# First batch of a fused attention and feed-forward kernel: attention times v in float32, shared exponentials, normalising on GpSimd, and weights converted in wider steps

## The chip, the cores and the metric

The kernel runs on one core of one Trainium2 chip. The metric is the device time of one launch in microseconds (us). Engines are called as the profile calls them: PE (TensorE, the matrix engine), PEld (its weight load), DVE (VectorE), ACT (ScalarE), POOL (GpSimd) and SP (SyncE, which only issues DMAs here).

## The reference

Attention with keys and values averaged over 8 neighbours, then a two-layer feed-forward net with a leaky ReLU. `q`, `k` and `v` are float32 [8 batches, 8 heads, 576, 64]; the weights are float64, 512 x 2048 and 2048 x 512.

```python
k_p = k.reshape(B, H, Sp, 8, D).mean(axis=3)          # Sp = 72
v_p = v.reshape(B, H, Sp, 8, D).mean(axis=3)
scores = (1 / sqrt(D)) * matmul(q, k_p.transpose(0, 1, 3, 2))
scores = scores - max(scores, axis=-1)
attn = exp(scores);  attn = attn / (sum(attn, axis=-1) + 1e-09)
x = matmul(attn, v_p).transpose(0, 2, 1, 3).reshape(4608, 512)
h = x @ w_in
out = maximum(0.01 * h, h) @ w_out                    # 4608 x 512, float32
```

## The kernel before

**Feed-forward net.** Nine chunks of 512 tokens, 16 parts of 128 hidden units each. For a chunk and a part, `m1` makes 12 matmuls of 512 columns into `ph`, and `m2` 12 more into the four sums `acc`. Each float32 factor is a high and a low half (`xh`, `xl`; halves of the weights; `gh`, `gl`), and of the four products three are made. The chunk of batch 0 is begun with parts 0 to 7 (run 0), then comes all of batch 1's chunk (run 1), then batch 0's parts 8 to 15, then the rest. The first matmul of a part in run 0 needs all four full tiles of batch 0's attention.

**Weights.** They come as float64 and are rebuilt from their two 32-bit words (`bits`): two steps on ACT (L183, L184) and three on DVE (L185, L186, L189) give a float32 `t`; ACT casts the high half (L193) and DVE subtracts it for the low half (L194). `convert(i, f)` does it for part f, i = 0 for `w_in` and i = 1 for `w_out`, 512 elements in each partition, in two steps, `head` and `tail`. Words wait in the space of weights that are converted later (`spare`), `t` in a buffer with the tag `o`. `convert_to(n)` sets how many steps have been written out by a given point.

**Attention.** A batch has five tiles of queries (four of 128, one of 64) and two groups of four heads. The string `FIRST` is the order by hand for batch 0: `lk` and `lv` pool keys and values, `ku` and `vu` place them, `q2` transposes tile 2 of the queries, `sa21` makes scores, maxima and exponentials of tile 2, group 1, `sb21` its normalising, `pu21` its transposing into `pT`, `au01` attention times v of piece 0, group 1, and `c` is one conversion step. Batch 1 goes between the matmuls of run 0; its pooling is on POOL. Exponentials are four ACT instructions a group, one for each head, each with its sum. `pT` and `v` are split into halves, with four reduced-precision matmuls (L467 to L470) for each pair of heads. Tiles 2 and 3 of batch 0 are normalised on DVE (`NORM_DVE`), the others on POOL.

**Order.** PE's instructions stay in the order in which the program is written. On the other engines a scheduler orders them when the kernel is built, and from then on each engine works its own list in order.

Of the kernel before, what the change touches and what calls it, by code (L numbers as in the profile page):

```python
# [24 lines left out]
def tile_pooled_attention_ffn(  # L25
# [54 lines left out]
    four = ctx.enter_context(tc.tile_pool(name="four", bufs=4))  # L80
# [36 lines left out]
    v_lo = const.tile([P, NK, 2, D], F32R, name="v_lo")  # L117
# [25 lines left out]
    NORM_DVE = (2, 3)  # L143

    def spare(f, i, shape, dtype, name):

        return wts.tile(shape, dtype, tag=f"w{i}_{f}", name=name)

    def stage(f):

# [3 lines left out]
        for i in range(2):
            shape = [P, DM, 2]
            if slot > f:
                t = spare(slot, i, shape, I32, f"w{i}_bits{f}")
            else:
                t = two.tile(shape, I32, tag="raw", name=f"w{i}_bits{f}")
            if i == 0:  # L160
                nc.sync.dma_start(
                    t.rearrange("p (k f) w -> p k f w", k=NK), w_in[:, :, f * P : (f + 1) * P, :]
                )
            else:
                nc.sync.dma_start(t, w_out[:, f, :, :])
            bits[i, f] = t

    def convert(i, f):

        st = {}  # L170

        def head():
            b = bits.pop((i, f))
            low, high = b[:, :, 0], b[:, :, 1]
            ws[i, f] = spare(f, i, [P, 2, DM], F32R, f"w{i}_{f}")
            t = five.tile([P, DM], I32, tag="o", name=f"w{i}_t{f}")
            st["w"] = t.bitcast(F32)
# [13 lines left out]
        def tail():  # L191
            w, t = ws[i, f], st["w"]
            nc.scalar.copy(w[:, 0, :], t)  # L193
            nc.vector.tensor_tensor(w[:, 1, :], t, w[:, 0, :].bitcast(F32), op=ALU.subtract)  # L194
# [169 lines left out]
    def q_unit(b, t, qr):  # L364
# [5 lines left out]
        nc.scalar.copy(qT[:, :, :n], pq[:, :, :n])  # L370
# [15 lines left out]
    def s_unit(b, t, g, qT):  # L386
# [14 lines left out]
        nc.vector.tensor_reduce(out=mx[:n], in_=scv[:n], axis=AX.X, op=ALU.max, negate=True)  # L401
        for h in range(4):
            ins = nc.scalar.activation(  # L403
                e[:n, h, :], scv[:n, h, :], AF.Exp, bias=mx[:n, h : h + 1],
                accum_out=sm[:n, h : h + 1],
            )
# [4 lines left out]
    def norm_unit(b, t, g, e, sm):  # L411
        n = tiles[b][t][1]
        eng = nc.vector if b == 0 and t in NORM_DVE else nc.gpsimd
        nc.vector.tensor_scalar_add(sm[:n], sm[:n], 1e-9)
        nc.vector.reciprocal(sm[:n], sm[:n])  # L415
        at = wide(b, t, g, "at", [3, P]) if wide_at(b, t, "at") else three.tile([P, 3, P], F32, tag="at", name=f"at{b}_{t}_{g}")
        eng.tensor_tensor(  # L417
# [3 lines left out]
        ins = eng.tensor_tensor(  # L421
# [16 lines left out]
    def p_unit(b, t, g, at, pc, o):
# [5 lines left out]
        nc.scalar.copy(pc["hi"][:, :, o : o + n], pp[:, 0:2, :n])
# [11 lines left out]
    def av_unit(b, j, g, pc):  # L456
# [3 lines left out]
        for i in range(2):  # L460
# [7 lines left out]
            nc.tensor.matmul(pa, vh, pc["lo"][:, i, :w], start=False, stop=False)  # L468
            nc.tensor.matmul(pa, vl, pc["hi"][:, i, :w], start=False, stop=False)  # L469
# [204 lines left out]
    def m2(k):  # L674
# [176 lines left out]
```

## Time and profile before

| | |
|---|---|
| three runs | 1009.0, 1004.41, 1011.04 us; median 1009.0 |
| profiled execution | 1006.54 us, span 1004.8 us |
| busy share of the span | PE 95%, PEld 77%, DVE 37%, ACT 43%, POOL 18% |
| mean granted clock of PE | 0.982 |
| chain that ended last | PE 88%, DVE 5%, ACT 4% |
| DMA | 57.44 MB, mean 57 GB/s |

The profile has one execution. A row of the order of time is: start in us from the span's start, duration, engine, line, operation, what it writes `<-` what it reads, shapes, how many; in brackets the idle time before it and what ended that. Durations of neighbours on one engine overlap a little, so the price of an instruction in a dense stretch is the distance from one start to the next.

### The profile page before, as it was taken

How to read it: one execution, taken by the hardware profiler on the slowest of the kernel's cores; microseconds unless marked ns; L12 is line 12 of the kernel's file. 1: busy time of each engine (PE TensorE's matmuls, PEld its weight loads, DVE VectorE, ACT ScalarE, POOL GpSimd, SP SyncE). 2: the span in 40 equal slices, each digit the busy share in tenths (PEclk: the TensorE clock that was granted, in tenths of full speed). 3: DMA queues.
4: the chain of work that ended last, by engine and by line, in shares of the span. 5: the costliest groups of instructions: out<-in, count | busy, mean ns of one | idle time of the engine just before them, and what ended most of it. 6: DMA issues, size and time to landing. Idle time of an engine off the chain costs nothing.

```text
span 1004.8 us, 12738 instructions
## 1 busy us (share of the span) xinstructions
PE 952.5 (95%) x4536; PEld 778.1 (77%) x4536; DVE 371.5 (37%) x902; ACT 428.2 (43%) x1386; POOL 177.4 (18%) x292
## 2 busy tenths in 40 slices
PE   4468899999999999999999999999999999999998
PEld 3457678888787778888887888788877888788886
DVE  5998639323432322233232333233223322221111
ACT  4677766234433343434343434344443433322221
POOL 3602200401116610132013301220110100100000
PEclk9689999999999999999999999999999999999999
DMA  9955311312033400121022202110100010001001
GB/s 241 267 171 149 88 60 42 103 34 69 1 104 101 105 11 17 58 74 32 6 64 58 58 1 69 46 29 1 58 22 11 1 48 1 1 1 42 0 1 42
DMA packets 65006, 57.44 MB, mean 57 GB/s; under 512 B 39856, under 2 KB 48048, under 8 KB 64944
## 3 DMA queue, kind: packets, MB, share of 16 engines
q1 hardware_dynamic: 64944, 56.64, 19.8%
q8 instruction: 36, 0.59, 0.3%
q14 instruction: 26, 0.21, 0.1%
HBM read 46.14 MB, written 10.49 MB: 56 GB/s over the span
## 4 chain that ended last, share of the span: by engine, by line
PE 88%; DVE 5%; ACT 4%; issue 1%; DMA 1%; SPq 1%; POOL 0%; DVEq 0%; ACTq 0%; POOLq 0%
PE ph L661 13%; PE acc L685 13%; PE ph L663 13%; PE ph L662 13%; PE acc L687 13%; PE acc L686 13%; PE pss L393 4%; PE pp L442 3%; PE pq L368 1%; ACT e L403 1%; PE pa L468 1%; PE pa L467 1%; PE pa L470 1%; PE pa L469 1%; SPq L240 1%
## 5 line engine op out<-in xcount | busy, mean ns | idle before, releaser
L661 PE MATMUL ph<-xh,w 128*128 128x512 f32 x576 | 235.8, 409 | 0.0
L685 PE MATMUL acc<-w,gh 128*128 128x512 f32 x576 | 233.7, 406 | 0.0
L663 PE MATMUL ph<-xh,w 128*128 128x512 f32 x576 | 226.3, 393 | 0.0
L662 PE MATMUL ph<-xl,w 128*128 128x512 f32 x576 | 226.1, 393 | 0.0
L687 PE MATMUL acc<-w,gl 128*128 128x512 f32 x576 | 225.7, 392 | 0.0
L686 PE MATMUL acc<-w,gh 128*128 128x512 f32 x576 | 225.5, 392 | 0.0
L670 DVE TENSOR_TENSOR gl<-ph,gh 128x512 fp32r<-128x512 f32 x144 | 99.4, 690 | 263.2 <-ACT gh L669 262.3
L666 ACT ACTIVATE ph<-ph 128x512 f32<-128x512 f32 x144 | 84.2, 585 | 250.4 <-PE ph L663 250.3
L403 ACT ACTIVATE e<-pss,red 128x72 f32<-128x72 f32 (+1 forms) x320 | 98.2, 320 | 115.5 <-DVE red L401 115.3
L417 POOL TENSOR_TENSOR at<-e,red 128x256 f32<-128x256 f32 (+1 forms) x76 | 47.4, 624 | 543.7 <-DVE red L415 267.8
L663 PEld LDWEIGHTS ph<-xh,w 128*128 128x128 f32 x576 | 108.7, 189 | 24.0
L687 PEld LDWEIGHTS acc<-w,gl 128*128 128x128 f32 x576 | 108.4, 188 | 23.8
L685 PEld LDWEIGHTS acc<-w,gh 128*128 128x128 f32 x576 | 108.5, 188 | 22.3 <-issue 1.6
L661 PEld LDWEIGHTS ph<-xh,w 128*128 128x128 f32 x576 | 108.8, 189 | 21.9 <-issue 1.4
L686 PEld LDWEIGHTS acc<-w,gh 128*128 128x128 f32 x576 | 108.7, 189 | 19.7
L662 PEld LDWEIGHTS ph<-xl,w 128*128 128x128 f32 x576 | 108.9, 189 | 19.1
L669 ACT CAST gh<-ph 128x512 fp32r<-128x512 f32 x144 | 85.4, 593 | 3.1
L401 DVE TENSOR_REDUCE red<-pss 128x4 f32<-128x288 f32 (+1 forms) x80 | 36.1, 453 | 94.3 <-PE pss L393 93.2
L403 ACT ACTIVATION_READ_ACCUMULATOR e<-pss,red 128x1 f32 (+1 forms) x320 | 65.4, 204 | 0.0
L393 PEld LDWEIGHTS pss<-kT,qT 128*128 128x128 f32 (+1 forms) x320 | 47.1, 183 | 14.4 <-ACT qT L370 4.9
L393 PE MATMUL pss<-kT,qT 128*128 128x144 f32 (+1 forms) x320 | 53.8, 295 | 4.1 <-ACT qT L370 4.1
L448 DVE TENSOR_TENSOR pT_lo<-pp,pT_hi 128x256 fp32r<-128x256 f32 (+1 forms) x80 | 31.7, 396 | 66.0 <-ACT pT_rem L445 65.3
(93 smaller groups left out, 844.1 us busy)
## 6 DMA issues: line engine op xcount, KB each, us to landing
out_dram<-o SPq DMA_DIRECT2D x35, 256.0 KB, 2.9
q<-in_q_dram SPq DMA_DIRECT2D x32, 256.0 KB, 3.9
w_bits<-in_moe_w_in_dram SPq DMA_DIRECT2D x16, 512.0 KB, 3.7
w_bits<-in_moe_w_out_dram SPq DMA_DIRECT2D x16, 512.0 KB, 3.5
k0raw<-in_k_dram SPq DMA_DIRECT2D x16, 256.0 KB, 3.7
k1raw<-in_k_dram SPq DMA_DIRECT2D x16, 256.0 KB, 4.4
v0raw<-in_v_dram SPq DMA_DIRECT2D x16, 256.0 KB, 3.8
v1raw<-in_v_dram SPq DMA_DIRECT2D x16, 256.0 KB, 5.6
```

What stands on the lines that cost most here:

```text
L393: nc.tensor.matmul(sc[:n, 2 * SP * i : 2 * SP * (i + 1)], qT[:, p, :n], kT[:, p, :, :].rearrange("d i s -> d (i s)"), start=True, stop=True,)
L403: ins = nc.scalar.activation(e[:n, h, :], scv[:n, h, :], AF.Exp, bias=mx[:n, h : h + 1], accum_out=sm[:n, h : h + 1],)
L417: eng.tensor_tensor(at[:n, 0:2, :].rearrange("a i (h s) -> a (i h) s", h=2), e[:n, :, 0:MAIN], sm[:n].unsqueeze(2).broadcast_to([n, 4, MAI ...
L661: nc.tensor.matmul(ph, w[:, 0, ks], xh[kk], start=kk == 0, stop=False)
L662: nc.tensor.matmul(ph, w[:, 0, ks], xl[kk], start=False, stop=False)
L663: nc.tensor.matmul(ph, w[:, 1, ks], xh[kk], start=False, stop=kk == NK - 1)
L666: nc.scalar.activation(ph, ph, AF.Prelu, alpha=0.01)
L669: casts.append(nc.scalar.copy(gh, ph))
L670: nc.vector.tensor_tensor(gl, ph, gh.bitcast(F32), op=ALU.subtract)
L685: nc.tensor.matmul(a, gh[:, r], hi, start=first, stop=False)
L686: nc.tensor.matmul(a, gh[:, r], lo, start=False, stop=False)
L687: nc.tensor.matmul(a, gl[:, r], hi, start=False, stop=last)
```

## The change

All of it concerns batch 0 and the conversion of weights.

- `v` of batch 0 is kept whole in float32 (`v_first`), and `pT` too; each pair of heads takes two full float32 matmuls. The low half of `pT` is gone for batch 0, and the remainder of `pT` is one DVE instruction instead of one on ACT and one on DVE. The low half of `v` gets its own tile, set to zero on POOL before batch 1.
- Tiles 0 and 1 take one exponential a group: DVE subtracts the maximum, ACT takes one exponential of 288 elements, DVE sums. Reciprocals of both groups of a tile are taken together, out of a buffer `reds` of which there are two. All normalising is on POOL, and batch 1's pooling is issued after the last one of tile 3. Batch 0's `qT` is copied by DVE instead of ACT.
- The parts 1 to 11 convert `w_in` and `w_out` together, 1024 elements at a time; their `t` is in a buffer of the tag `raw` (two buffers, which batch 1's `kremraw` and `vremraw` use before). `FIRST` and the counts of `convert_to` are set for the fewer steps.

```diff
-        "lk ku q0 q1 sa00 sb00 sa01 sb01 lv sa10 sb10 sa11 sb11 q2 sa20 sa21 vu pu00 pu10 c c q3 "
-        "pu01 pu11 c sb20 sb21 au00 sa30 sa31 c au01 c pu20 pu21 sb30 sb31 c c pu30 pu31 c au10 au11 "
-        "c q4 c c / sa40 sa41 sb40 sb41 c c c"
+        "lk ku q0 q1 sa00 sa01 sb00 sb01 lv sa10 sa11 sb10 sb11 q2 sa20 sa21 vu pu00 pu10 sb20 sb21 q3 "
+        "pu01 pu11 c c sa30 sa31 au00 sb30 sb31 au01 c pu20 pu21 c pu30 pu31 c au10 au11 "
+        "c q4 c / sa40 sa41 sb40 sb41 c c"
...
-    NORM_DVE = (2, 3)
+    NARROW = (0, 12, 13, 14, 15)
...
+            low, high = (b[..., k] for k in range(2))
+            if i is None:
+                t = two.tile([P, 2, DM], I32, tag="raw", name=f"t{f}")
             else:
-                t = two.tile(shape, I32, tag="raw", name=f"w{i}_bits{f}")
+                t = five.tile([P, DM], I32, tag="o", name=f"w{i}_t{f}")
...
+            w = ws[f] if i is None else ws[f][:, i]
+            hi, lo = (w[..., k, :] for k in range(2))
+            nc.scalar.copy(hi, st["t"])
+            nc.vector.tensor_tensor(lo, st["t"], hi.bitcast(F32), op=ALU.subtract)
...
+            if b == 0:
+                nc.scalar.mul(v_first[r, :, i, :], sums[r], 1.0 / POOL)
+                continue
...
-        nc.scalar.copy(qT[:, :, :n], pq[:, :, :n])
+        (nc.scalar.copy if b else nc.vector.tensor_copy)(qT[:, :, :n], pq[:, :, :n])
...
+                reds[t] = two.tile([P, 2, 2, 4], F32, tag="reds", name=f"reds{t}")
+            red = reds[t][:, :, g]
...
+        if b == 0 and t < 2:
+            nc.vector.tensor_tensor(
+                e[:n], scv[:n], mx[:n].unsqueeze(2).broadcast_to([n, 4, SP]), op=ALU.add
+            )
+            nc.scalar.activation(e[:n], e[:n], AF.Exp)
+            nc.vector.tensor_reduce(out=sm[:n], in_=e[:n], axis=AX.X, op=ALU.add)
+            return e, sm
...
-        eng = nc.vector if b == 0 and t in NORM_DVE else nc.gpsimd
-        nc.vector.tensor_scalar_add(sm[:n], sm[:n], 1e-9)
-        nc.vector.reciprocal(sm[:n], sm[:n])
+        if b > 0 or g == 0:
+            r = sm[:n] if b else reds[t][:n, 1]
+            nc.vector.tensor_scalar_add(r, r, 1e-9)
+            nc.vector.reciprocal(r, r)
...
+        if b == 0:
+            anchor["act"] = nc.scalar.copy(pc["hi"][:, :, o : o + n], pp[:, 0:2, :n])
+            nc.vector.tensor_scalar_mul(rem, pp[:, 2, :n], m_lo)
+            return
...
+            if b == 0:
+                vw = v_first[:, p, :, :].rearrange("a i d -> a (i d)")
+                nc.tensor.matmul(pa, vw, pc["hi"][:, i, :w], start=True, stop=False)
+                nc.tensor.matmul(pa, vr.bitcast(F32), pc["rem"][:, :w], start=False, stop=True)
...
-    for i, f in [(i, f) for f in range(NF) for i in range(2)]:
+    for i, f in [(i, f) for f in range(NF) for i in ((0, 1) if f in NARROW else (None,))]:
...
-    att[1]["lk"]()
-    att[1]["lv"]()
+    with tc.issue_after(anchor["pool"].ins):
+        att[1]["lk"]()
+        att[1]["lv"]()
...
-                convert_to(14 + 2.8 * f)
+                convert_to(10 + 1.5 * f)
             elif n == 1:
-                convert_to(36 + 3 * f)
+                convert_to(22 + (1.5 if f < 8 else 3) * f)
```

How the lists of the engines move, at three places. Numbers in names are running numbers of buffers; lines are those of each kernel.

DVE before, from the first maximum of tile 0 on (`red_0_0` is tile 0, group 0):

```order
L401 TENSOR_REDUCE red_0_0_224<-pss_0_0_220 128x4
L228 TENSOR_TENSOR v1raw_139<-v1raw_139 128x2x256
L401 TENSOR_REDUCE red_0_1_239<-pss_0_1_235 128x4
L228 TENSOR_TENSOR vremraw_142<-vremraw_142 64x256
L228 TENSOR_TENSOR v1raw_139<-v1raw_139 128x2x128
L401 TENSOR_REDUCE red_1_0_263<-pss_1_0_259 128x4
L401 TENSOR_REDUCE red_1_1_277<-pss_1_1_274 128x4
L414 TENSOR_SCALAR red_0_0_224<-red_0_0_224 128x4
```

DVE now at the same place (`reds_215` is tile 0, `reds_249` tile 1; `v0raw` and `kremraw` are now the names of the buffers that also hold v's second half and v's remainder):

```order
L395 COPY qT_1_209<-pq_1_204 128x512
L431 TENSOR_REDUCE reds_215<-pss_0_0_211 128x4
L244 TENSOR_TENSOR v0raw_135<-v0raw_135 128x2x256
L434 TENSOR_TENSOR e_0_0_214<-pss_0_0_211,reds_215 128x288
L244 TENSOR_TENSOR kremraw_129<-kremraw_129 64x256
L431 TENSOR_REDUCE reds_215<-pss_0_1_220 128x4
L244 TENSOR_TENSOR v0raw_135<-v0raw_135 128x2x128
L431 TENSOR_REDUCE reds_249<-pss_1_0_245 128x4
L431 TENSOR_REDUCE reds_249<-pss_1_1_254 128x4
L244 TENSOR_TENSOR kremraw_129<-kremraw_129 64x128
L438 TENSOR_REDUCE reds_215<-e_0_0_214 128x4
```

Before, the next step after the four maxima is the preparation of tile 0's reciprocal (L414). Now copies, subtractions of the maximum (L434) and sums (L438) stand before it, twenty instructions behind the first add of `v0raw`.

POOL before, at the end of tile 1's normalising and the start of batch 1's pooling:

```order
L417 TENSOR_TENSOR at_1_271<-e_1_262,red_1_1_277 128x256
L421 TENSOR_TENSOR at_1_271<-e_1_262,red_1_1_277 128x128
L228 TENSOR_TENSOR k0raw_162<-k0raw_162 128x2x256
L228 TENSOR_TENSOR k0raw_162<-k0raw_162 128x2x128
L228 TENSOR_TENSOR k1raw_165<-k1raw_165 128x2x256
```

POOL now, from the same place (tile 2's result has tile 1's name, since they share a buffer; tile 3's has the name `e_1`):

```order
L457 TENSOR_TENSOR at_1_263<-e_1_248,reds_249 128x256
L461 TENSOR_TENSOR at_1_263<-e_1_248,reds_249 128x128
L457 TENSOR_TENSOR at_1_263<-e_2_278,reds_279 128x256
L461 TENSOR_TENSOR at_1_263<-e_2_278,reds_279 128x128
L457 TENSOR_TENSOR at_1_263<-e_2_278,reds_279 128x256
L461 TENSOR_TENSOR at_1_263<-e_2_278,reds_279 128x128
L457 TENSOR_TENSOR e_1_248<-e_2_278,reds_361 128x256
L461 TENSOR_TENSOR e_1_248<-e_2_278,reds_361 128x128
L457 TENSOR_TENSOR e_1_248<-e_2_278,reds_361 128x256
L461 TENSOR_TENSOR e_1_248<-e_2_278,reds_361 128x128
L244 TENSOR_TENSOR k0raw_157<-k0raw_157 128x2x256 x2
```

Eight instructions for tiles 2 and 3 have come between tile 1 and the pooling.

DVE before, at the last halves of x (`xl`) of piece 1 and the maxima of tile 4; conversions of parts 1 and 2 stand between:

```order
L185 TENSOR_SCALAR w_t_569<-w_bits_180 128x512
L194 TENSOR_TENSOR w_1_493<-w_t_494,w_1_493 128x512
L485 TENSOR_TENSOR xl_2_408<-pa_1_2_539,xh_2_404 128x256
L189 ISA w_t_519<-w_bits_178,w_t_519 128x1024
L485 TENSOR_TENSOR xl_3_409<-pa_1_3_546,xh_3_405 128x256
L186 SCALAR_TENSOR_TENSOR w_t_569<-w_bits_180,w_t_569 128x512
L401 TENSOR_REDUCE red_4_0_581<-pss_4_0_577 64x4
```

DVE now, at the same place:

```order
L531 TENSOR_TENSOR xl_2_384<-pa_1_2_458,xh_2_380 128x256
L395 COPY qT_4_479<-pq_4_474 128x4x64
L531 TENSOR_TENSOR xl_3_385<-pa_1_3_463,xh_3_381 128x256
L431 TENSOR_REDUCE reds_493<-pss_4_0_489 64x4
L431 TENSOR_REDUCE reds_493<-pss_4_1_499 64x4
L454 TENSOR_SCALAR reds_493<-reds_493 64x8
L455 RECIPROCAL reds_493<-reds_493 64x8
L198 TENSOR_SCALAR t_425<-bits_150 128x1024
L199 SCALAR_TENSOR_TENSOR t_425<-bits_150,t_425 128x1024
```

All conversion of part 1 (`t_425`) has moved behind tile 4's reciprocals; before, parts 1 and 2 were nearly done there.

More of the change, by code (lines that the diff above doesn't have):

```diff
@@ L79, in tile_pooled_attention_ffn @@
     three = ctx.enter_context(tc.tile_pool(name="three", bufs=3))
-    four = ctx.enter_context(tc.tile_pool(name="four", bufs=4))
+    small = ctx.enter_context(tc.tile_pool(name="small", bufs=3))
     ps_acc = ctx.enter_context(tc.tile_pool(name="ps_acc", bufs=1, space=PSUM))
@@ L116, in tile_pooled_attention_ffn @@
     v_hi = const.tile([P, NK, 2, D], F32R, name="v_hi")
-    v_lo = const.tile([P, NK, 2, D], F32R, name="v_lo")
+    v_first = one.tile([P, NK, 2, D], F32, tag="v_lo", name="v_first")
     v_rem = const.tile([P, 2, 4, D], F32R, name="v_rem")
@@ L142, in tile_pooled_attention_ffn @@
     BEHIND = 3
-    NORM_DVE = (2, 3)
+    NARROW = (0, 12, 13, 14, 15)
+    halves = {}
     def spare(f, i, shape, dtype, name):
-        return wts.tile(shape, dtype, tag=f"w{i}_{f}", name=name)
+        if f not in halves or i in halves[f][1]:
+            halves[f] = wts.tile([P, 2, 2 * DM], dtype, tag=f"w{f}", name=name), set()
+        t, taken = halves[f]
+        taken.add(i)
+        n = int(_np.prod(shape[1:]))
+        names = [f"x{k}" for k in range(len(shape) - 1)]
+        return t[:, i, :n].rearrange(
+            f"p ({' '.join(names)}) -> p {' '.join(names)}", **dict(zip(names, shape[1:]))
+        )
     def stage(f):
@@ L153, in stage @@
         slot = NF - 1 if f == NF - 2 else NF - 1 - f % SPARE
[L154 to L158, printed above, removed]
-                t = two.tile(shape, I32, tag="raw", name=f"w{i}_bits{f}")
[L160 to L166, printed above, removed]
+        if slot > f:
+            both = wts.tile([P, 2, DM, 2], I32, tag=f"w{slot}", name=f"bits{f}")
+            bits[f] = both, [both[:, i] for i in range(2)]
+        else:
+            bits[f] = None, [
+                two.tile([P, DM, 2], I32, tag="raw", name=f"w{i}_bits{f}") for i in range(2)
+            ]
+        nc.sync.dma_start(
+            bits[f][1][0].rearrange("p (k f) w -> p k f w", k=NK), w_in[:, :, f * P : (f + 1) * P, :]
+        )
+        nc.sync.dma_start(bits[f][1][1], w_out[:, f, :, :])
     def convert(i, f):
@@ L172, in head @@
         def head():
[L173 to L177, printed above, removed]
+            b = bits[f][0] if i is None else bits[f][1][i]
+            low, high = (b[..., k] for k in range(2))
+            if i is None:
+                t = two.tile([P, 2, DM], I32, tag="raw", name=f"t{f}")
+            else:
+                t = five.tile([P, DM], I32, tag="o", name=f"w{i}_t{f}")
+            st["t"] = t.bitcast(F32)
             after = casts[-BEHIND] if len(casts) >= BEHIND else anchor.get("act")
@@ L336, in place_k @@
         nc.vector.tensor_scalar_mul(kT[64:128, :, 1, MAIN:], prv[64:128, :, 1, :], KSCALE)
+    v_los = []
     def place_v(b, sums, rem):
+        if b == 1:
+            v_los.append(one.tile([P, NK, 2, D], F32R, tag="v_lo", name="v_lo"))
+            nc.gpsimd.memset(v_los[0].bitcast(F32), 0.0)
         for i in range(2):
             r = slice(64 * i, 64 * i + 64)
+            if b == 0:
+                nc.scalar.mul(v_first[r, :, i, :], sums[r], 1.0 / POOL)
+                continue
             nc.scalar.mul(v_hi[r, :, i, :], sums[r], 1.0 / POOL)
             nc.vector.scalar_tensor_tensor(
-                v_lo[r, :, i, :], sums[r], 1.0 / POOL, v_hi[r, :, i, :].bitcast(F32),
+                v_los[0][r, :, i, :], sums[r], 1.0 / POOL, v_hi[r, :, i, :].bitcast(F32),
                 op0=ALU.mult, op1=ALU.subtract,
```

54 lines of the change are left out of this document (27 added, 27 removed).

## The prediction

> **What bounds the kernel now.** I read the page first, for where TensorE (PE) is not full, then the busy time by stretch, then the order of time of each engine in the first 140 us.
>
> ```profile
> span 1004.8 us, 12738 instructions
> PE   4468899999999999999999999999999999999998
> DVE  5998639323432322233232333233223322221111
> ```
>
> A digit is 25 us. PE is full but for the first eight slices, and there DVE is the full engine. The table by stretch (columns: length, busy us of PE, PEld, DVE, ACT, POOL, clock, DMA share, GB/s) shows it closer:
>
> ```profile
> 30.00:40.00 10.00, 2.65 (x13) 2.25 (x13) 10.00 (x14) 7.17 (x28) 9.88 (x10) 0.70 1.07 284
> 40.00:50.00 10.00, 4.65 (x19) 3.93 (x20) 10.00 (x26) 5.01 (x14) 3.77 (x8) 0.50 0.88 263
> ...
> 60.00:70.00 10.00, 7.81 (x34) 6.09 (x32) 8.79 (x21) 8.77 (x20) 0.00 (x0) 0.76 0.36 106
> 70.00:80.00 10.00, 7.19 (x40) 5.70 (x39) 9.47 (x23) 6.65 (x20) 0.09 (x1) 1.00 0.68 200
> 80.00:90.00 10.00, 8.10 (x34) 6.50 (x35) 8.52 (x20) 7.91 (x28) 2.57 (x4) 0.83 0.59 175
> 90.00:100.00 10.00, 9.28 (x51) 7.64 (x50) 7.14 (x19) 8.61 (x30) 3.23 (x6) 1.00 0.37 114
> ...
> 140.00:150.00 10.00, 10.00 (x46) 8.29 (x45) 2.77 (x7) 6.19 (x14) 0.00 (x0) 1.00 0.26 101
> ```
>
> From 30 to 50 us DVE has no gap and PE works 7.3 of 20 us; from 140 us PE has none. Three first matmuls of parts mark the way:
>
> ```profile
> 53.02 0.50 PE L661 MATMUL ph<-xh,w 128*128 128x512 f32 x1
> ...
> 64.56 0.61 PE L661 MATMUL ph<-xh,w 128*128 128x512 f32 x1
> ...
> 134.51 0.39 PE L661 MATMUL ph<-xh,w 128*128 128x512 f32 x1
> ```
>
> These are part 0, part 1, and the first part of batch 1's chunk. What comes after 134.51 is PE's own work and the change leaves it alone. So the question is how many us earlier that row comes.
>
> **Why DVE is full.** POOL's pooling of batch 1's k and v runs in the same time:
>
> ```profile
> 28.15 2.64 POOL L228 TENSOR_TENSOR k0raw<-k0raw 128x512 f32<-128x512 f32 x2 [5.71 <-DMA k0raw<-in_k_dram]
> ...
> 37.65 1.27 POOL L228 TENSOR_TENSOR v1raw<-v1raw 128x512 f32<-128x512 f32 x1
> 38.88 0.72 POOL L228 TENSOR_TENSOR vremraw<-vremraw 64x256 f32<-64x256 f32 x1
> ...
> 43.27 0.49 POOL L234 TENSOR_TENSOR vremsum<-vremraw 64x64 f32<-64x64 f32 x1
> ```
>
> ```profile
> 37.30 4.12 DVE L414 TENSOR_SCALAR red<-red 128x4 f32<-128x4 f32 x1
> ```
>
> An add of 4 elements takes 4.12 us while POOL runs one instruction behind the other. Part of DVE's fullness is therefore interference.
>
> **The change, part by part.** Prices are distances from one start to the next where DVE is dense and POOL rests:
>
> ```profile
> 33.53 0.44 DVE L401 TENSOR_REDUCE red<-pss 128x4 f32<-128x288 f32 x1
> 33.90 0.74 DVE L485 TENSOR_TENSOR xl<-pa,xh 128x256 fp32r<-128x256 f32 x2
> ...
> 45.38 0.41 DVE L448 TENSOR_TENSOR pT_lo<-pp,pT_hi 128x256 fp32r<-128x256 f32 x1
> 45.71 0.33 DVE L452 SCALAR_TENSOR_TENSOR pT_rem<-pp,marks,pT_rem 128x128 fp32r<-128x128 f32 x1
> ...
> 48.69 0.41 DVE L185 TENSOR_SCALAR w_t<-w_bits 128x512 int32<-128x512 int32 x1
> 49.02 0.68 DVE L189 CUSTOM_DVE_ANT_0 w_t<-w_bits,w_t 128x1024 uint16<-128x1024 uint16 x1
> 49.62 0.68 DVE L194 TENSOR_TENSOR w<-w_t,w 128x512 fp32r<-128x512 f32 x1
> 50.23 0.21 DVE L348 SCALAR_TENSOR_TENSOR vremparts<-vremsum,vremparts 64x64 fp32r<-64x64 f32 x1
> ```
>
> So 288 elements from PSUM take 0.37, 256 take 0.33, 512 take 0.60 (0.33 for L185), and 0.06 of each is fixed.
>
> *Conversion in one go.* A part costs DVE now 2 x (0.33 + 3 x 0.60) = 4.26; with 1024 elements 0.60 + 3 x 1.14 = 4.0. No row has 1024 elements; the bounds are twice the 512 price (no gain) and that minus 0.06 (0.26 us a part), and I take the latter, since 256 to 512 shows it. For parts 3 to 7, which lie in the bound stretch, that is 1.3 us.
>
> *Shared exponentials and the start.* DVE's list is now longer at the start. From the landing of v's second half on:
>
> ```profile
> 15.03 0.69 DVE L228 TENSOR_TENSOR v1raw<-v1raw 128x512 f32<-128x512 f32 x1 [0.70 <-DMA v1raw<-in_v_dram]
> ...
> 21.82 0.46 DVE L401 TENSOR_REDUCE red<-pss 128x4 f32<-128x288 f32 x1 [0.22 <-PE pss L393]
> ```
>
> ```profile
> 18.25 0.62 POOL L417 TENSOR_TENSOR at<-e,red 128x256 f32<-128x256 f32 x1 [3.11 <-DVE vremsum L234]
> ...
> 22.04 0.40 POOL L421 TENSOR_TENSOR at<-e,red 128x128 f32<-128x128 f32 x1
> ```
>
> Up to tile 0's reciprocal stand 11 instructions of 288 elements (4 shifts, 3 maxima, 4 sums; 4.07), the first v add (0.61), a copy of qT (0.60, priced as 512 elements), two adds of 256 (0.66), three small ones (0.60) and four tiny ones (0.76): 7.3 us, so normalising starts at 22.3 instead of 18.25. Four pairs on POOL took 18.25 to 22.44, 4.2 us. Tile 2's maxima reuse tile 0's small buffer (two buffers of `reds`) and wait for the second pair, 22.3 + 2.1 = 24.4, against 21.82. So the exponentials of tile 2 start 2.5 us later. This is a wait that the change adds; behind it in DVE's queue stand qT of tile 3 and the scaling of `pT`, which PE needs.
>
> *From there ACT leads.*
>
> ```profile
> 22.37 0.32 ACT L403 ACTIVATE e<-pss,red 128x72 f32<-128x72 f32 x1 [1.04 <-DVE red L401]
> ...
> 24.76 0.41 ACT L444 CAST pT_hi<-pp 128x256 fp32r<-128x256 f32 x1
> ...
> 25.59 0.76 ACT L183 ACTIVATE w_bits<-w_bits 128x512 f32<-128x512 f32 x1
> 26.17 0.74 ACT L184 ACTIVATE w_bits<-w_bits 128x512 int32<-128x512 uint32 x1
> ```
>
> Eight exponentials take 2.4, a conversion step of 512 elements 0.58, a copy of 256 by half of that 0.28. From 24.9: tile 2 (2.4), three `pT` copies (0.8), four steps of part 0 (2.3), tile 3 with two `xh` between (2.9): 33.3. Reciprocals 0.35, two pairs on POOL 2.1: tile 3 is normalised at 35.7. In the kernel before, that was here:
>
> ```profile
> 44.57 0.28 DVE L421 TENSOR_TENSOR at<-e,red 128x128 f32<-128x128 f32 x1
> ...
> 58.01 0.43 DVE L185 TENSOR_SCALAR w_t<-w_bits 128x512 int32<-128x512 int32 x1
> ```
>
> The four tiles are through 9 us earlier, as DVE neither subtracts low halves (8 x 0.33) nor normalises, and as POOL's pooling now stands behind the last normalising instead of beside it.
>
> *What is late next.* The pooling, 28.15 to 43.76 = 15.6 us before, starts at 35.7. Alone I make it 13.0: four instructions of 512 elements at 1.23 (37.65 to 38.88), eight of 256 at 0.69 (the 0.72 of the 38.88 row, less the same overlap of 0.03), five of 128 at 0.42 (by the line through the two) and the last at 0.49. I take 13.0, as DVE has little to do then; the other end is 15.6. Two things wait for it. The normalising of tile 4 is behind it on POOL. And the converted words `t` of parts 1 and 2 now use buffers of the tag `raw`, which hold batch 1's k and v remainders until the pooling's last sums: only three small instructions come after, so DVE can't begin part 1 before 35.7 + 13.0 - 1.3 = 47.4, and idles.
>
> *The sum.* From 47.4 DVE has parts 1 and 2 to do, 2 x 4.0: 55.4. The kernel before begins part 3 at 58.01 with one subtraction of 0.60 still owed: 58.6. That is 3.2 us gained at equal work. Then 1.3 from the wide steps. From 60 to 100 us DVE idled 1.21 + 0.53 + 1.48 + 2.86 = 6.1 us in the kernel before; with conversions owed, some of it is filled. The ends are 0 and 6.1; I take 2.0, since most of these gaps are waits for ACT's steps on the same chain, which stay. **Sum: 6.5 us** earlier. The profiled execution took 1006.54 (span 1004.8 and 1.7 around it), so 1000.0; the median of the three runs is 1009.0, 2.5 higher, so **1002.5**.
>
> *Attention times v in float32.* It costs PE more and DVE less. PE's prices at full clock:
>
> ```profile
> 75.41 0.65 PE L393 MATMUL pss<-kT,qT 128*128 128x144 f32 x4
> 75.81 0.49 PE L661 MATMUL ph<-xh,w 128*128 128x512 f32 x1
> ...
> 102.97 0.28 PE L468 MATMUL pa<-pT_lo,v_hi 128*128 128x256 f32 x1
> 103.08 0.28 PE L469 MATMUL pa<-pT_hi,v_lo 128*128 128x256 f32 x1
> ```
>
> Two whole float32 matmuls of 144 columns (two records each) take 0.40, so 256 columns 0.36; a reduced one of 256 takes 0.12. Eight groups: 16 x 0.36 - 32 x 0.12 = +1.9 us. PE idles 5.3 us between 40 and 50 us, which covers it; uncovered it costs 1.9, double at half clock. The Trainium skill, "FP8 and Floating Point Precision", section "TensorE Precision Notes", speaks against this edit: true float32 makes four passes through the array. By that it is 16 x 0.48 - 32 x 0.12 = +3.8 us, still under the same cover; the pss rows, at three passes by the column, bear it out in part.
>
> **The rivals.** (a) *The lead at part 1 lasts.* Part 1 can start at about 53.4 (47.4, t of part 1 and most of part 2, the subtraction), 11 us before 64.56. Should DVE's gaps fill wholly, the gain is 3.2 + 1.3 + 6.1 = 10.6: 998.4. For it speaks PE's idle share of 19 to 28% from 60 to 90; against it that DVE then owes the conversions which the kernel before had done by 58 us.
> (b) *Slower: POOL holds DVE.* Small adds from SBUF to SBUF (tile 3's and tile 4's `reds`, the first step of a part) now stand beside POOL's dense list, as the 4.12 us row did. Each such stall is worth up to 4.0; pooling stretched to 15.6 adds 2.6. Two stalls and the stretch: 10.6 - 6.5 = 4.1 slower, 1013. It decides from 6.5 us of stall on. Against: DVE is nearly idle during the pooling, so the stall may hide.
> The Trainium skill, "SBUF — State Buffer", section "Who interferes with whom", has it that whichever engine issues first keeps the shared port pair for a whole instruction and the other blocks until its end. By that rule one add waits at most the 1.3 us of one POOL instruction, two cost 2.6, and (b) ends at 1008; the 4.12 us row, across five POOL instructions, does not agree.
> (c) *The work is only put off.* If the gaps stay and a longer step in front of a short one costs PE 2 us, the gain is 0 to 3: 1007.5.
>
> **How the numbers follow.** Forecast 0.46, (a) 0.27, (c) 0.17, (b) 0.10. The range: (a) on the low side, 998, less the 4.6 by which the fastest of the three runs lies under the median, 993; (b) on the high side, 1012. One per cent, about what a measurement can tell from no change, is 10 us: all of (a) and a little of the forecast are beyond it (0.31); of (b) with a third stall 0.05 is slower than that; 0.64 lies between.
>
> **What would show it.** POOL's first normalising near 22.3 and its pooling from about 36 to 49; part 1's conversion on DVE not before 47; the first matmul of part 1 near 53; of batch 1's first part near 128. I am wrong if DVE's stalls beside POOL exceed 1 us, if `pT` and `xh` come later than 42 us, or if the gaps of PE between 60 and 100 are larger than before.

## The result, and the profile after

The changed kernel takes 1017.11 us (median of 4 runs, 1016.34 to 1019.08); the kernel before, beside it, 1007.14. The ratio is 1.0100, interval 1.0076 to 1.0123: one per cent slower, where 1002.5 was forecast. The page of the profiled execution:

```profile
span 1014.9 us, 12595 instructions
PE   4678989999999999999999999999999999999998
DVE  6699557113332332232232333233223321221111
```

A digit is 25 us. From 25 to 50 us PE's rises from 4 to 6 and DVE's falls from 9 to 6, which fits the earlier part 0 and DVE's wait for the pooling. From 150 us to the last slice PE's line is all nines in both, and that is the trap: it hides what is lost there. The three rows that marked the way, in the order of time of PE:

```profile
45.37 0.50 PE L707 MATMUL ph<-xh,w 128*128 128x512 f32 x1
...
59.08 0.79 PE L707 MATMUL ph<-xh,w 128*128 128x512 f32 x1
...
136.22 0.39 PE L707 MATMUL ph<-xh,w 128*128 128x512 f32 x1
```

Part 0 begins 7.65 us earlier than before (53.02), part 1 5.48 earlier (64.56), and batch 1's first part 1.71 **later** (134.51). The span is 10.1 us longer, so 8.4 us are lost behind that row, where the prediction had put nothing. The table by stretch (length, PE busy, instructions, clock, DMA share, GB/s) shows it, first for the kernel before, then for the changed one:

```profile
150.00:215.00 65.00, 65.00 (x288) 1.00 0.24 70
```

```profile
150.00:215.00 65.00, 65.00 (x283) 1.00 0.27 75
```

In both PE is busy all the time at full clock, but the changed kernel gets through five matmuls fewer. The order of time shows why. Before, every matmul starts 0.22 to 0.23 us behind the last:

```profile
153.35 0.39 PE L663 MATMUL ph<-xh,w 128*128 128x512 f32 x1
153.58 0.39 PE L685 MATMUL acc<-w,gh 128*128 128x512 f32 x1
153.80 0.39 PE L686 MATMUL acc<-w,gh 128*128 128x512 f32 x1
154.03 0.39 PE L687 MATMUL acc<-w,gl 128*128 128x512 f32 x1
```

In the changed kernel the same four:

```profile
155.40 0.40 PE L709 MATMUL ph<-xh,w 128*128 128x512 f32 x1
155.63 0.40 PE L731 MATMUL acc<-w,gh 128*128 128x512 f32 x1
155.87 0.40 PE L732 MATMUL acc<-w,gh 128*128 128x512 f32 x1
156.10 0.39 PE L733 MATMUL acc<-w,gl 128*128 128x512 f32 x1
```

The distances are 0.23, 0.24 and 0.23. A part of 24 matmuls, first row to first row, takes 5.440 us before and 5.553 now, in each of the next 15 parts. PE's instructions and their forms are the same in this stage, and it waits for nothing in either kernel. Batch 1's chunk loses 1.8 us in this way and the last chunk 1.7; the chunks between, with attention's matmuls among theirs, lose 0.3 to 0.9 each. One thing that differs is where the operands lie in SBUF, the memory that the engines read: the two new tiles `reds` (64 bytes a partition each) stand in the pool `two`, and all that is laid out behind them, `gh` and `gl` among it, lies 128 bytes higher than before.

### The profile page after: what moved, and what is told of

The parts are those of the page before. It is cut to its first block, busy times and chain, and to the rows that moved or that the text cites. A ratio compares the mean times of both kernels' runs of the same rounds, so it can differ in the third digit from the quotient of the medians.

```text
span 1014.9 us, 12595 instructions
## 1 busy us (share of the span) xinstructions
PE 965.1 (95%) x4536; PEld 780.4 (77%) x4536; DVE 359.8 (35%) x841; ACT 417.8 (41%) x1310; POOL 183.8 (18%) x301
## 4 chain that ended last, share of the span: by engine, by line
PE 85%; DMA 4%; DVE 3%; ACT 3%; SPq 2%; issue 2%; POOL 1%; DVEq 0%; ACTq 0%; POOLq 0%
PE acc L731 13%; PE ph L707 13%; PE ph L709 12%; PE acc L733 12%; PE acc L732 12%; PE ph L708 12%; PE pss L418 3%; PE pp L480 2%; PE pq L393 1%; DMA v0raw<-in_v_dram 1%; ACT e L441 1%; DMA k0raw<-in_k_dram 1%; DMA bits<-in_moe_w_out_dram 1%; SPq L256 1%; DVE t L202 1%
## 5 line engine op out<-in xcount | busy, mean ns | idle before, releaser
L457 POOL TENSOR_TENSOR at<-e,red 128x256 f32<-128x256 f32 (+1 forms) x70 | 43.8, 626 | 527.1 <-DVE red L455 276.5
L441 ACT ACTIVATE e<-pss,red 128x72 f32<-128x72 f32 (+1 forms) x280 | 86.0, 320 | 112.8 <-DVE red L431 111.6
L431 DVE TENSOR_REDUCE red<-pss 128x4 f32<-128x288 f32 (+1 forms) x70 | 31.8, 454 | 94.7 <-PE pss L418 93.1
L441 ACT ACTIVATION_READ_ACCUMULATOR e<-pss,red 128x1 f32 (+1 forms) x280 | 57.0, 204 | 0.0
L489 DVE TENSOR_TENSOR pT_lo<-pp,pT_hi 128x256 fp32r<-128x256 f32 (+1 forms) x70 | 27.8, 397 | 65.5 <-ACT pT_rem L488 65.0
```

The source lines that it names most:

```text
L441: ins = nc.scalar.activation(e[:n, h, :], scv[:n, h, :], AF.Exp, bias=mx[:n, h : h + 1], accum_out=sm[:n, h : h + 1],)
L457: nc.gpsimd.tensor_tensor(at[:n, 0:2, :].rearrange("a i (h s) -> a (i h) s", h=2), e[:n, :, 0:MAIN], sm[:n].unsqueeze(2).broadcast_to([n, ...
```

## The experiments: the stage that the change left alone

All runs are timed beside the kernel before, and their ratios are to it. Rivals for the 8.4 us: the place of `gh` and `gl`, or the new layout of the weights (one tile of 8 KB a part instead of two of 4 KB).

**e1_reds_last**, the changed kernel with `reds` laid out last:

```diff
+    redp = ctx.enter_context(tc.tile_pool(name="redp", bufs=2))
-                reds[t] = two.tile([P, 2, 2, 4], F32, tag="reds", name=f"reds{t}")
+                reds[t] = redp.tile([P, 2, 2, 4], F32, tag="reds", name=f"reds{t}")
```

> The changed kernel with the small tile reds moved from the pool two to a pool of its own behind all others; gh, gl, the outputs and the q buffers then lie 128 bytes lower, exactly where they were before the change, and nothing else differs. Place theory: the 8.4 us that the stage after batch 1's first matmul lost come from gh and gl lying 128 bytes off their old place; a part of 24 matmuls then takes 5.44 us again instead of 5.553, and the median falls by about 8 us, to 1009 (1008 to 1010.5). Layout theory: they come from the weights lying in one tile of 8 KB a part instead of two of 4 KB; then 5.553 stays and the median stays at 1017. Start theory: the first matmul of batch 1's first part comes at 136 in either case, 1.7 us later than before.

Measured: 1009.61 us, ratio 1.0017 (1.0000 to 1.0033). The stretch is back at the old count, and batch 1's first row stays where the changed kernel has it:

```profile
136.17 0.39 PE L708 MATMUL ph<-xh,w 128*128 128x512 f32 x1
```

```profile
150.00:215.00 65.00, 65.00 (x288) 1.00 0.25 73
```

So 128 bytes of placement are worth 7.5 us of the median (8.4 by the ratios), and the new weight layout nothing.

**e2_four_first** and **e3_three_early** are the kernel before with one line of pool creation moved, no instruction changed:

```diff
+    four = ctx.enter_context(tc.tile_pool(name="four", bufs=4))
     three = ctx.enter_context(tc.tile_pool(name="three", bufs=3))
-    four = ctx.enter_context(tc.tile_pool(name="four", bufs=4))
```

> The kernel before with one line moved: the pool four (128 bytes, the statistics red) is created ahead of the pool three, so that at, gh and gl lie 128 bytes higher, as in the changed kernel; no instruction differs. Place theory: a part of 24 matmuls takes 5.55 us instead of 5.44 and the median rises by 7 to 9 us, to 1014 to 1016. Layout theory and a theory of another chip: 5.44 and 1007, no difference.

> The kernel before with the pool three (at, gh, gl) created ahead of the pool two, so that gh and gl lie at a multiple of 512 bytes; weights stay at 256 past a multiple of 512; no instruction differs. If what counts is that gh lies as the weights do within 512 bytes, a part takes 5.5 us or more and the median rises by 7 us or more, to 1014. If any multiple of 256 bytes will do, nothing changes: 5.44 and 1007.

Measured: e2 1014.32 us, 1.0067 (1.0044 to 1.0091); e3 1007.60, 1.0001 (0.9987 to 1.0015). The loss can be put into the kernel before. Its table row for e2:

```profile
150.00:215.00 65.00, 65.00 (x283) 1.00 0.25 69
```

**e11_all128** and **e12_x128** ask whether a place is bad in itself or only beside another. Both are the kernel before with the pool `four` created earlier: ahead of the weights in e11, between the weights and x in e12.

> The kernel before with one line moved: the pool four (128 bytes) is created ahead of the pool of the weights, so that weights, q and x buffers, gh and gl all lie 128 bytes higher, and how they lie to each other stays; no instruction differs. If the place itself counts (multiples of 256 bytes are good, 128 past one is bad), a part of 24 matmuls takes at least the 5.553 us of the run with gh alone moved, and the median rises by 8 us or more, since every operand now lies badly. If only the distance between gh and the weights counts, a part takes 5.44 and nothing changes.

> The kernel before with one line moved: the pool four (128 bytes) is created between the weights and the pool one, so that x as well as gh and gl lie 128 bytes higher, and the weights stay. Distance theory: an operand pair whose starts differ by 128 bytes within 256 is slow; now both halves of a part have one (weights with x, gh with weights), so a part of 24 matmuls takes 5.55 to 5.65 us with no run of 227 ns pitches left in it, and the median rises by 7 to 14 us. If only gh's place counts, the part takes 5.553 with its four pitches of 227 as in the changed kernel. If the distance is not what counts, 5.44.

Measured: e11 1010.23 us, 1.0019 (1.0001 to 1.0037), with 5.440 us in 13 of the 15 parts (one takes 6.503 and the next 5.577, much as in e6, where gh and gl lie as before); its small excess fits these two and a start that came at 136.69; e12 1021.13, 1.0128 (1.0104 to 1.0152), with 5.593 a part:

```profile
150.00:215.00 65.00, 65.00 (x280) 1.00 0.29 83
```

The table puts the seven together. Places are bytes past a multiple of 512 in a partition, as the built programs list them; each matmul loads one operand of a pair as its stationary side and streams the other.

| kernel | weights | x | gh, gl | apart in `ph` | apart in `acc` | us a part |
|---|---|---|---|---|---|---|
| before, e1 | 256 | 0 | 256 | 256 | 0 | 5.440 |
| e3 | 256 | 0 | 0 | 256 | 256 | 5.440 |
| e11 | 384 | 128 | 384 | 256 | 0 | 5.440 |
| after, e2 | 256 | 0 | 384 | 256 | 128 | 5.553, 5.554 |
| e12 | 256 | 128 | 384 | 128 | 128 | 5.593 |

In these runs the distance between the two operands decides, and not the place of either: 0 and 256 are good, 128 is slow. (Whether it is the two operands of one matmul, or the one that is streamed and the one that is loaded next, they can't tell: it is the same distance.) In the changed kernel the twelve `acc` matmuls start 228 to 241 ns apart, and the first seven distances between the `ph` matmuls behind them are 224 to 236 as well, before 227 returns; so the loss outlasts the badly placed pairs. In e12, where both halves of a part are 128 apart, no matmul starts 0.227 behind the last any more (0.229 and 0.234 to 0.238 by turns). Distances other than these three were not tried.

## The experiments: the start

Here the changed kernel should have been 6.5 us ahead at batch 1's first row and is 1.7 behind. First rows of parts in us, from PE's order of time:

| run | part 0 | part 1 | part 2 | part 5 | batch 1 | ratio (interval) |
|---|---|---|---|---|---|---|
| before | 53.02 | 64.56 | 73.95 | 103.80 | 134.51 | 1 |
| e1 | 45.49 | 59.06 | 67.25 | 102.78 | 136.17 | 1.0017 (1.0000 to 1.0033) |
| e4 remainders elsewhere | 54.57 | 68.33 | 77.71 | 108.14 | 141.88 | 1.0067 (1.0044 to 1.0090) |
| e5 wait filled | 44.87 | 58.28 | 69.64 | 103.95 | 135.77 | 1.0031 (1.0013 to 1.0048) |
| e6 narrow | 54.40 | 65.42 | 74.91 | 104.51 | 136.82 | 1.0018 (1.0002 to 1.0034) |
| e7 pooling set free | 52.92 | 68.63 | 78.01 | 111.58 | 145.35 | 1.0071 (1.0051 to 1.0091) |
| e8 tile 4 on DVE | 45.12 | 56.97 | 67.96 | 103.07 | 136.47 | 1.0001 (0.9985 to 1.0017) |
| e9 later steps | 44.18 | 58.60 | 71.60 | 104.62 | 133.48 | 0.9984 (0.9969 to 0.9998) |
| e10 and narrow from 9 | 45.25 | 57.94 | 70.46 | 102.77 | 131.15 | 0.9971 (0.9952 to 0.9989) |
| e13 little pooling | 48.56 | 59.31 | 69.07 | 102.38 | 131.31 | 0.9947 (0.9929 to 0.9966) |
| e14 e10 with e8 | 43.98 | 56.61 | 67.53 | 106.83 | 135.21 | 0.9996 (0.9977 to 1.0016) |

All rows from e4 down build on e1, so that the place costs nothing. Read the columns down: part 0 begins anywhere from 44 to 54.6, and part 5 at 102.4 to 104.6 in all but e4, e7 and e14. A lead at part 0 is worth almost nothing by itself.

**e4_krem** takes away the wait for the raw buffers:

```diff
     RAW = {
+        (1, "krem"): (11, 0), (1, "vrem"): (11, 1),
```

> The run with reds moved, and besides the remainders of batch 1's k and v staged in the slot of part 11's weights instead of the two raw buffers, so that the conversion of part 1 need not wait for batch 1's pooling. If that wait (the step of the prediction that put part 1's conversion at 47.4) costs the start its gain, DVE begins part 1's conversion 4 to 5 us before 49.8, the later waits of TensorE for DVE shrink and the first matmul of batch 1's first part comes at 130 to 133 instead of 136, the median 3 to 6 us under the run with reds moved alone. If DVE is held by GpSimd's pooling or TensorE by other waits, under 2 us change.

Measured: 1014.25 us, 4.6 over e1. DVE did begin early, and stood beside GpSimd's pooling. Its rows and GpSimd's:

```profile
38.16 2.19 DVE L200 SCALAR_TENSOR_TENSOR t<-bits,t 128x1024 int32<-128x1024 int32 x1
...
40.79 3.72 DVE L203 CUSTOM_DVE_ANT_0 t<-bits,t 128x2048 uint16<-128x2048 uint16 x1
```

```profile
40.89 2.48 POOL L246 TENSOR_TENSOR v0raw<-v0raw 128x512 f32<-128x512 f32 x2
43.33 1.76 POOL L246 TENSOR_TENSOR kremraw<-kremraw 64x256 f32<-64x256 f32 x1
```

The same form on GpSimd in the changed kernel, where DVE rests:

```profile
39.19 0.72 POOL L244 TENSOR_TENSOR kremraw<-kremraw 64x256 f32<-64x256 f32 x1
```

The wide steps take 2.19 and 3.72 where a step in a quiet stretch takes 1.14, and the halving add 1.76 instead of 0.72. The rows read like turns: the step begun at 40.79 lasts as long as the two adds of GpSimd that run to 43.37 and its own 1.14 together, and the add begun at 43.33 about as long as the rest of that step and its own 0.7. The last halves of x, for which part 0 waits, stand behind them on DVE: part 0 slips 9 us. The wait that the prediction had booked as a loss was a shelter.

**e5_fill**, **e6_narrow**, **e7_poolfree**, **e8_norm4**:

```diff
 # e5
+        if (b, t, g) == (0, 4, 0):
+            for _ in range(14):
+                nc.tensor.matmul(pp.rearrange("a p x -> a (p x)"), ws[0][:, 0, 0, 0:P], x_parts(0)[0][0], start=True, stop=True)
 # e6, with the c steps of FIRST doubled for parts 1 and 2
+    NARROW = tuple(range(16))
+                convert_to(14 + 2.8 * f)
+                convert_to(36 + 3 * f)
 # e7
-    with tc.issue_after(anchor["pool"].ins):
 # e8
+        eng = nc.vector if b == 0 and t == 4 else nc.gpsimd
```

> The run with reds moved, and 14 matmuls of 512 columns more on TensorE, whose result is overwritten, just ahead of tile 4's transposes, where TensorE waits 3.83 us for GpSimd; they take 14 x 0.227 = 3.2 us and leave the output as it is. Clock theory of the start: that wait is followed by a half clock (0.50 from 51.6 to 61.8) under the matmuls of part 0 and 1; with the wait filled this stretch goes, the first matmul of batch 1's first part comes at 131 to 133 instead of 136.2 and the median at 1005 to 1007 instead of 1009.6. Late-conversion theory: VectorE sets the pace there, and the row comes at 135 to 137, the median within 1 us of 1009.6.

> The run with reds moved, with every part converted in two steps of 512 elements as before the change, on the old schedule of steps (14 + 2.8 and 36 + 3 a part); its t buffers are then the output buffers and not the raw ones. Wide-step theory: the steps of 1.14 us stand ahead of short ones for which TensorE waits (kT 1.87, v_rem 2.42, xl 1.53 us); with narrow steps these waits shrink by half, the first matmul of batch 1's first part comes at 132 to 134 instead of 136.2, the median at 1006 to 1008. By the prediction's prices the wide steps save 1.3 us: then it comes at 137 to 138, the median at 1010 to 1012. And since t no longer waits for the raw buffers, conversion stands beside GpSimd's pooling: by what the run with the remainders moved showed, that alone costs 3 to 6 us.

> The run with reds moved, without the order that puts batch 1's pooling behind tile 3's normalising on GpSimd; the scheduler then sets it among the normalising of tiles 2 and 3, as it stood before the change. Late-conversion theory: pooling ends at 46 to 47 instead of 49.5, VectorE begins part 1 some 3 us earlier, and the first matmul of batch 1's first part comes at 132 to 134, the median at 1006 to 1008. Contention theory: the pooling then stands beside VectorE's work on part 0 and holds up tile 3, part 0 starts at 49 to 52 instead of 45.5, and nothing is gained or up to 3 us lost.

> The run with reds moved, with tile 4 alone normalised on VectorE instead of GpSimd. GpSimd takes 1.0, 1.37, 1.05 and 1.37 us for it (49.9 to 54.6) and VectorE's first wide steps beside it 1.4 to 1.6 instead of 1.14. If this meeting costs the start something, VectorE pays 1.4 us for the normalising and saves some 1.3, TensorE's wait at 51 shrinks by 1 us and the second one of 1.0 goes: the first matmul of batch 1's first part comes at 134 to 135.5, the median 1 to 2 us lower. If not, within 1 us of 1009.6.

e5: the forecast of the clock theory fails. In the changed kernel a wait of 3.97 us stands ahead of a half clock, and in e5 both shrink, but batch 1's row comes only 0.4 earlier than in e1 and the time is no better. A half clock follows in e5 from 68 us on (the last row), behind a wait of 4.6 us for VectorE's `kT` that lasts 2.0 in the changed kernel. The changed kernel, then e5:

```profile
47.00:51.00 4.00, 0.03 (x2) 1.00 0.01 2
51.00:62.00 11.00, 8.82 (x29) 0.53 0.52 168
```

```profile
47.00:51.00 4.00, 2.92 (x13) 1.00 0.01 2
51.00:62.00 11.00, 7.44 (x35) 0.84 0.59 191
...
68.00:72.00 4.00, 3.12 (x10) 0.50 1.02 351
```

e6: narrow steps lose the whole lead at part 0 (54.40) and still end where e1 ends; the conversions run beside the pooling again, and the two effects that the expectation set against each other are not told apart. e7: pooling set free is 5.4 us slower than e1 by the ratios, more than the 3 that the contention theory allowed, so to put it behind tile 3's normalising was right. e8: no earlier row; its ratio is 0.0016 below e1's with overlapping intervals, and e14 gained nothing from the same edit. It is not shown to help.

**e9_pace**:

```diff
-                convert_to(10 + 1.5 * f)
+                convert_to(9 + 1.43 * f)
-                convert_to(22 + (1.5 if f < 8 else 3) * f)
+                convert_to(19 + (1.5 if f < 8 else 3) * f)
```

> The run with reds moved, with the conversion steps called for later in the program: 9 + 1.43 f instead of 10 + 1.5 f in the first stretch, 19 instead of 22 at the head of the second. The changed kernel has 9 parts converted at 95.2 us and 10 at 103.8, the kernel before 8 at 95.8 and 9 at 114.5, while only 8 are needed before batch 1's first part. Pace theory: VectorE is full there (37.5 of 40 us from 60 to 100), so the 4 to 8 us of work done too soon hold up attention; called for later, batch 1's first part starts at 132 to 134 instead of 136.2, the median at 1006 to 1008 instead of 1009.6. If attention's own chain sets the pace from part 4 on (all runs reached part 4 at 103 to 104.5 though part 0 started at 45 or at 54), nothing moves: 135.5 to 137 and 1009 to 1010.

Measured: 1006.21 us; batch 1's row at 133.48, 2.7 earlier than in e1. (The row that the text calls part 4's is part 5's.) The groups of DVE's low-half subtractions up to 104 us, for the kernel before, the changed one and e9:

```profile
L194 DVE TENSOR_TENSOR w<-w_t,w 128x512 fp32r<-128x512 f32 x17 | 13.0, 773 | 1.4 <-ACT w L193 1.4
```

```profile
L210 DVE TENSOR_TENSOR w<-t,w 128x1024 fp32r<-128x1024 f32 x9 | 11.1, 1231 | 1.5 <-ACT w L209 1.4
L210 DVE TENSOR_TENSOR w<-w_t,w 128x512 fp32r<-128x512 f32 x2 | 1.9, 945 | 0.0
```

```profile
L211 DVE TENSOR_TENSOR w<-t,w 128x1024 fp32r<-128x1024 f32 x7 | 8.7, 1242 | 0.5 <-ACT w L210 0.5
L211 DVE TENSOR_TENSOR w<-w_t,w 128x512 fp32r<-128x512 f32 x2 | 1.8, 924 | 0.0
```

A part is two rows of 512 or one of 1024: 8.5 parts before, 10 in the changed kernel, 8 in e9 (its ninth follows at 104.40, just behind the cut; by batch 1's row it is 10, 12 and 11). The stretches say what it did to DVE (columns: length, then busy us of PE, PEld, DVE, ACT, POOL, clock, DMA), the changed kernel and e9:

```profile
60.00:100.00 40.00, 30.77 (x145) 23.80 (x143) 37.61 (x62) 30.63 (x77) 8.43 (x11) 0.89 0.62 199
```

```profile
60.00:100.00 40.00, 31.54 (x140) 24.88 (x138) 32.11 (x54) 28.71 (x74) 6.17 (x11) 0.83 0.53 172
```

DVE is full 94% of that stretch in the changed kernel, partly with weights that PE needs only after batch 1's eighth part; in e9 it is 80%. So the pace is worth 2.7 us at the row, but not quite as the expectation had it. Part 5 begins 1.8 us later than in e1, and the gain lies wholly behind it: from there to batch 1's row e9 takes 28.9 us and e1 33.4, with PE's waits 2.7 instead of 5.6 and no half clock (0.66 from 112 to 117 in e1). Which of the steps called for later does this was not taken apart; e9 moves those of the first stretch and those at the head of the second together.

**e10_pace_n9**: e9 with `NARROW = (0, *range(9, 16))` and `convert_to(19 + 3 * f)`.

> The run before this one, with parts 9 to 15 converted in narrow steps of 512 elements (the changed kernel: parts 0 and 12 to 15). Wide-step theory of the last stretch: from the second half of part 7 to batch 1's first part all runs with wide steps took 13.99 us, the kernel before and the run with narrow steps 12.77; with parts 9 to 11 narrow this stretch takes 12.8 again, so the first row comes 1.2 us earlier than in the run before this one. If not, 13.99 and no difference.

Measured: 1005.65 us. The stretch named (it runs from the first row of part 7) takes 12.51 us, but 12.98 in e9 already, so the pace had mended it; the rest of the 2.3 us comes before part 5, and the medians of e9 and e10 are not apart. The theory of wide steps is left undecided. **This version is faster than both kernels**, if by little: 0.9971 (0.9952 to 0.9989) of the kernel before, 0.1 to 0.5 per cent. It is the best of several, and e14, one edit further, is not apart from the kernel before.

**e13_nopool** and **e14_pn9_norm4**:

```diff
 # e13, for batch 1 alone
-        for w in (256, 128):
+        for w in ():
```

> The run with reds moved and later conversion steps, without the two halving adds that precede each last sum in batch 1's pooling, so that GpSimd's pooling of batch 1 is 6 instructions instead of 18 (this leaves out 6 of the 8 neighbours that are averaged in batch 1). Hold theory of the lost lead: part 0 starts 8.8 us earlier than before, but VectorE begins part 1 only at 49.8 since the raw buffers are held until the pooling's end; now pooling ends near 40.5, VectorE begins part 1 by 42, the lead of 6 to 8 us lasts to part 2, and batch 1's first part starts at 126 to 129 instead of 133.5; the median 4 to 7 us lower than 1006.2. If attention's chain or DMA bounds the stretch after part 0, it starts at 132 to 134 and nothing is gained.

> The run with reds moved, later conversion steps and narrow steps from part 9 on, with tile 4 normalised on VectorE besides. Alone that took 1.3 us off the median of the run with reds moved (1008.3 against 1009.6), about what three rounds tell apart, with the first row of batch 1 no earlier (136.5). If it is real, the median is 1004 to 1005; if not, 1005.5 to 1006.5.

Measured: e13 1004.58 us; by the ratios 3.7 under e9. Its kernel leaves out work of the pooling, so its time is a bound and not a version to use. DVE begins part 1 at 38.12 instead of 49.67 in e9, though part 0 then begins 4.4 us later, and the row of batch 1 comes at 131.31, 2.2 us earlier than in e9 and not 5 to 7. That much the pooling costs the start here. From part 5 to batch 1's row e13 takes 28.9 us, as e9 does, so what was gained was gained before part 5. What sets part 5 near 103 in runs that have no engine full there was not settled. e14: 0.9996 (0.9977 to 1.0016), no gain over e10.

## Why the prediction was wrong, step by step

**What held.** POOL's first normalising at 22.32 (22.3 forecast), pooling from 36.72 to 49.54 (35.7 to 48.7), 12.8 us long (13.0), DVE's conversion of part 1 not before 47 (49.78). Rows of the changed kernel:

```profile
22.32 0.61 POOL L457 TENSOR_TENSOR at<-e,reds 128x256 f32<-128x256 f32 x1 [6.88 <-DVE reds L455]
...
36.72 2.50 POOL L244 TENSOR_TENSOR k0raw<-k0raw 128x512 f32<-128x512 f32 x2
...
49.23 0.31 POOL L250 TENSOR_TENSOR vremsum<-vremraw 64x64 f32<-64x64 f32 x1
```

```profile
48.14 1.43 DVE L454 TENSOR_SCALAR reds<-reds 64x8 f32<-64x8 f32 x1 [2.22 <-ACT e L441]
...
49.78 0.69 DVE L198 TENSOR_SCALAR t<-bits 128x1024 int32<-128x1024 int32 x1
50.51 1.52 DVE L199 SCALAR_TENSOR_TENSOR t<-bits,t 128x1024 int32<-128x1024 int32 x1
...
52.75 1.63 DVE L202 CUSTOM_DVE_ANT_0 t<-bits,t 128x2048 uint16<-128x2048 uint16 x1
...
59.71 1.21 DVE L210 TENSOR_TENSOR w<-t,w 128x1024 fp32r<-128x1024 f32 x1
60.84 0.27 DVE L485 TENSOR_SCALAR pT<-pp,marks 128x64 f32<-128x64 f32 x1
```

The price of a wide step held where POOL rests (59.71 to 60.84 is 1.13).

**Float32 attention, a term put at nothing.** Its price lies between the prediction's two, 0.36 and 0.48: in the changed kernel's rows a whole float32 matmul of 256 columns (two records) takes 0.43 to 0.44, with a granted clock of 1.00 from 42 to 44 us.

```profile
41.44 0.60 PE L509 MATMUL pa<-pT,v_first 128*128 128x256 f32 x2
41.88 0.59 PE L510 MATMUL pa<-pT,v_rem 128*128 128x256 f32 x2
42.31 0.59 PE L509 MATMUL pa<-pT,v_first 128*128 128x256 f32 x2
42.74 0.59 PE L510 MATMUL pa<-pT,v_rem 128*128 128x256 f32 x2
```

Nor did PE's idle time cover it. The last eight of these matmuls keep PE busy without a gap from 37.97 to 43.27, at a clock of 0.50 from 38 to 40 us, and tile 4's scores and part 0 follow them in PE's order. Part 0 still began 7.65 us earlier, and no run takes this edit out, so what it costs at batch 1's row stays open.

**The step that failed most: "What comes after 134.51 is PE's own work and the change leaves it alone."** The instructions were left alone, their operands' places were not. 8.4 us of the profiled span, 7.5 of the median (e1). With that alone put right the median would lie inside the range (1009.61). The range itself ended at 1012, a little under the 1013 that rival (b) gave; the measured time lies beyond both.

**The sum of the start** missed by as much: 6.5 us were forecast at batch 1's row and 1.7 lost. "55.4 against 58.6 at equal work, 3.2 gained": parts 1 and 2 were done at 60.92, or 60.3 without the first step of part 3 that lies among them, so 1.7 were lost instead. DVE began 2.4 later than forecast, as pooling began 1.0 later and the add for tile 4's reciprocals (48.14) stood 1.43 us beside it where the one for tile 3 took 0.16; DVE's steps beside POOL's normalising of tile 4 then took 1.52 and 1.63; and other work, `gl` of part 0 above all, stood between. And the work up to 104 us was not equal: the new counts of `convert_to` called for 1.5 parts more by 104 us, at 4.0 us each by the prediction's price, in the stretch where DVE is full. The diff showed the numbers; they were read as a change of unit (fewer, wider steps) and never worked out in parts. e9 gives 2.7 us of that back at the row and 3.3 by the ratios. The terms of 1.3 for wider steps and 2.0 for filled gaps were swallowed by this: DVE's idle time from 60 to 100 us did fall, from 6.1 to 2.4, but the early work filled it.

**The signs.** All three of the prediction's signs of being wrong came, the second in part: a stall beside POOL of over 1 us (48.14), the last copies of `xh`, though not of `pT`, later than 42 us (ACT starts them at 42.51 and 43.37), and larger gaps of PE between 60 and 100 us (9.2 us idle against 7.6). Part 1's first row came at 59.08 and not near 53.

**The rivals.** (b), POOL holding DVE, was given 0.10 and is a real mechanism of this start (e4, e7), but the changed kernel largely dodges it with its hold: by the rows above it pays some 2.5 us, an estimate (1.3 at 48.14, and 1.2 by which the five steps from 49.78 to 55.65 exceed their quiet prices), where 6.5 were needed for (b) to decide. (c), work only put off, comes nearest for the start: a gain of 0 to 3 was forecast there and 1.7 lost. No rival had a loss in the long stage.

**Left open:** what sets part 5 near 103 us, and with it the 3 to 5.5 us by which even e10 and e9 stay behind the start that was forecast near 128.

## What to carry to other kernels

A change of buffers is a change of addresses for all that is laid out behind them: compare the places of the operands of the longest loop before and after. Here two operands of a matmul ran well 0 and 256 bytes apart (modulo 512) and badly at 128. Where a stage is PE-bound and looks untouched, take the distance of its matmuls from the order of time, not its busy share, which reads 65.00 of 65.00 either way. Counts that pace background work must be turned into units of work at a common time before two schedules are called equal.

## What the runs showed of the hardware

A pair of operands 128 bytes apart within 256 makes back-to-back matmuls of 512 columns start up to 241 ns apart instead of 227 (5.553 or 5.593 us for 24 instead of 5.440). The Trainium skill, "SBUF — State Buffer", section "Who interferes with whom", says that the stream of a matmul and the weight load have read ports of their own, independent, and that PE never waits on anyone. No other engine is needed for the loss here: one pool moved by 128 bytes brings it (e2), so PE's pace does depend on how its two operands lie to each other, and the measurement decides. That the two reads get in each other's way is inferred from this, not seen.

With operands well placed, too, the dense spacing is not there at once. Also in the kernel before, after matmuls of another shape, the next ones start (behind a first distance of 325 ns) up to 236 ns apart for some ten instructions:

```profile
345.16 0.65 PE L393 MATMUL pss<-kT,qT 128*128 128x144 f32 x4
345.55 0.49 PE L685 MATMUL acc<-w,gh 128*128 128x512 f32 x1
345.88 0.40 PE L686 MATMUL acc<-w,gh 128*128 128x512 f32 x1
346.11 0.40 PE L687 MATMUL acc<-w,gl 128*128 128x512 f32 x1
346.35 0.40 PE L685 MATMUL acc<-w,gh 128*128 128x512 f32 x1
```

A wide DVE step beside a dense list on GpSimd took up to 3.72 us instead of 1.14, and GpSimd's instruction 1.76 instead of 0.72 (e4): both lose, as if they took turns, so to overlap them gains less than either's idle time suggests.
